# Seven late turnings by transposing transfers, EV on 128 rows, zero fills as steps, and a new order, in a recurrent attention + squared-ReLU kernel

## The chip, the cores and the metric

The kernel runs on one core of one Trainium2 chip. The metric is device microseconds of one execution, the median of three runs of the kernel before: 245.29 us (245.1 to 246.02). One further execution was profiled; its page and its trace are what is read below.

## The reference

For each of 4 batches and 8 heads, a 40x40 state is carried over 768 steps; its output feeds a two-layer network with squared ReLU.

```python
B, H, S, D = 4, 8, 768, 40
for t in range(S):
    y[:, :, t] = einsum('bhd,bhde->bhe', r_t, state)
    Sa = einsum('bhde,bhe->bhd', state, a_t)
    state = state * w_t[:, :, None, :] - einsum('bhd,bhe->bhde', Sa, b_t)
    state = state + einsum('bhd,bhe->bhde', v_t, k_t)
x = y.transpose(0, 2, 1, 3).reshape(B * S, H * D)      # 3072 x 320
h = maximum(x @ w_in, 0)                               # 320 x 2048
out = (h * h) @ w_out                                  # 2048 x 320
```

Inputs and output are float32; the kernel multiplies in bf16 and sums in float32.

## The kernel before, in words

The 768 steps are cut into 12 chunks of 64. A chunk is worked for all 32 (batch, head) pairs at once; 64 steps of two batches fill the 128 partitions. `load`, `prep`, `rec`, `read` and `ffn` add the steps of a chunk `c` to a plan, and `weights` adds the loads and casts of the network's weights. The names of the steps, with the chunk behind them:

- `ldw`, `ldk`, `ldb`, `ldv`, `lda`, `ldr`: the loads of a chunk, two transfers of 160 KB each, on SP's queue. `lwi` (8), `lwl` (1) and `lwo` (8): the weights; `cwi`, `cwl`, `cwo` cast them to bf16 (WIN, WLAST, WOUT). `st`: a chunk's store.
- `ln`, `hi`, `lo`, `ci`, `cf`, then `ei`, `ex`, `ef`, `eg`, `exw`: cumulative decay, by logarithm, a product with a triangle of ones on TensorE (PE) and an exponential. `castA`, `castR`, `castV`, `castB`, `castK`, `mulKB`: the inputs to bf16, keys and b scaled by the decay.
- Turnings: TK, TA, TR, TV, TS and XT transpose tiles on PE through an identity; `tK`, `tA`, `tR`, `tV`, `tS`, `xt` copy the result out of PSUM on ACT or DVE. TK turns KB (keys and b, [128, 32, 64]) into KBT; TV turns VU (v and u, same shape) into VUT; TS turns the state STb into Sb. In chunks 0 to 3 they work on 128x128 (line 397), later on 64-row halves, 32 matmuls each (line 394). BK turns back in chunks 0 to 2.
- EN, CX (lines 675 to 694): the two triangles, per half g, masked by `mEN`, `mCX` on DVE. AS: a times state. EV: first triangle times v, into the same PSUM slot; `u0` copies it; NU multiplies again by the triangle; `u1` writes the result u into the other 64 rows of VU.
- SC and S: the new state, scaled by `s` into STb. RS and Y: the output, from r times Sb (that is, the state of the chunk before) and from CX times keys; `y`, `yd` scale it, XT turns it.
- F (256 rows of w_in, line 390) and FL (its last 64 rows) per quarter u of the 2048 columns, `f` the ReLU, `q` the square, O the second product, `o` the copy out. In the last chunk O is three parts, OA, OB, OC.

A PE step has an array shape: 128*128 (F, O, whole turnings), 64*128 by row halves (FL, EN, CX, ci, cf, 64-row turnings), 128*64 by column halves (AS, SC, S, RS, Y), or 64*64 quadrants (EV, NU).

The order is written out: the string ORDER lists every step with its engine (`PE2` also names one of four PSUM slots), `Plan.issue` emits them in that order, and each engine works through its own entries in that order. A step's declared reads and writes become waits. PE's order is thus fixed: if the next step's input is late, PE stands. SP's queue is as strict: a transfer whose input is late holds those behind it. The buffers VU and KB are three deep (`NK`), most others two.

Ahead of the plan, constants are made and padding is zeroed on DVE and POOL (lines 312 to 323). One line each for a turning's matmul and its copy:

```python
pe(f"TV {c}", *tmode(c), ms, reads=VU0 + VU1, writes=[hb], alloc=[hb])
evac(f"tV {c}", lambda s, n, hb=hb: turned_pairs(VUT[q2], hb, c, s, n),
     1024, [hb], [("VUT", q2)], [hb])
```

Of the kernel before, what the change touches and what calls it, by code (L numbers as in the profile page):

```python
# [86 lines left out]
ORDER = """SP ldw 0; SP ldk 0; SP ldb 0; SP ldw 1; ACT ln 0; DVE hi 0; DVE lo 0; SP lda 0; PE0 cf 0; POOL  # L87
castB 0; SP ldk 1; POOL castK 0; ACT eg 0; PE1 TK 0; SP ldb 1; ACT ln 1; PE2 ci 0; DVE tK 0 g0;
ACT ef 0; SP ldv 0; DVE tK 0 g1; POOL hi 1; ACT exw 0; ACT castA 0; SP lda 1; DVE lo 1; PE1 TA 0;
ACT castB 1; PE2 ci 1; SP ldw 2; DVE tA 0 g1; DVE tA 0 g0; PE0 EN 0 g1; ACT exw 1; PE1 cf 1; POOL  # L90
castV 0 g1; DVE mEN 0 g1; ACT castK 1; SP ldr 0; POOL castV 0 g0; PE2 EN 0 g0; ACT ef 1; PE3 BK 0;
# [18 lines left out]
TV 2; PE2 TS 1; DVE s 2 q0; ACT tV 2; SP lwo 0 x2; DVE s 2 q1; PE0 F 0 u2; DVE tS 1; SP lwo 0 x3;  # L110
PE FL 0 u2; ACT castR 2; SP ldv 3; PE1 RS 1; PE Y 1; ACT castA 3; PE2 FL 0 u3; ACT f 0 u2; PE F 0
u3; DVE mulKB 3 h0; POOL mulKB 3 h1; PE3 TA 3; DVE y 1; ACT f 0 u3; PE0 TR 2; DVE yd 1; DVE tA 3
g0; PE1 XT 1; ACT tRw 2; SP ldr 3; PE2 TK 3; DVE xt 1; ACT cwo 0 x2; DVE tA 3 g1; POOL cwo 0 x3;
PE1 FL 1 u1; DVE tK 3; SP ldw 4; PE F 1 u1; POOL q 0 u1; PE3 CX 2 g1; ACT f 1 u1; PE0 CX 2 g0; DVE
mCX 2 g1; PE2 F 1 u2; ACT castV 3 g0; POOL castV 3 g1; SP lwo 0 x4; PE FL 1 u2; DVE mCX 2 g0; PE3
EN 3 g0; ACT f 1 u2; PE1 F 1 u0; POOL castR 3; SP lwo 0 x5; DVE mEN 3 g0; POOL q 0 u0; PE0 EN 3
g1; SP ldk 4; PE FL 1 u0; PE2 RS 2; DVE mEN 3 g1; PE Y 2; PE3 AS 3; ACT ln 4; ACT f 1 u0; PE0 FL 1
u3; DVE hi 4; PE EV 3; DVE yd 2; DVE lo 4; PE F 1 u3; ACT u0 3; POOL cwo 0 x4; DVE y 2; SP lda 4;
PE NU 3; ACT f 1 u3; PE2 ci 4 h0; POOL cwo 0 x5; DVE u1 3 g0; PE1 TS 2; ACT ex 4 h0 g1; SP ldb 4;
POOL q 0 u2; ACT ei 4 h0; DVE u1 3 g1; PE0 O 0 u0; ACT ex 4 h0 g0; ACT tS 2; PE2 ci 4 h1; POOL q 0  # L120
u3; PE3 TV 3; SP lwo 0 x6; ACT ex 4 h1 g0; ACT ei 4 h1; PE1 SC 3; DVE tV 3; ACT ex 4 h1 g1; SP lwo
0 x7; PE S 3 g0; PE S 3 g1; POOL castA 4; SP ldw 5; PE2 TR 3; DVE s 3 q1; PE O 0 u1; ACT tRw 3;
DVE s 3 q0; POOL mulKB 4 h0; PE3 XT 2; PE2 CX 3 g0; ACT xt 2; PE1 cf 4; DVE mCX 3 g0; PE O 0 u2;
ACT ef 4; SP ldv 4; DVE mulKB 4 h1; ACT cwo 0 x6; PE2 TA 4; PE1 CX 3 g1; POOL cwo 0 x7; DVE tA 4
g1; PE3 TK 4; DVE tA 4 g0; POOL q 1 u1; ACT tK 4; PE O 0 u3; DVE mCX 3 g1; PE2 F 2 u0; SP ldw 6;
DVE o 0; ACT q 1 u2; PE3 F 2 u2; DVE q 1 u0; ACT ln 5; PE0 EN 4 g0; PE FL 2 u2; DVE mEN 4 g0; PE1
FL 2 u3; POOL hi 5; ACT f 2 u2; PE FL 2 u0; SP ldr 4; PE F 2 u3; POOL lo 5; ACT f 2 u0; PE3 RS 3;
DVE f 2 u3; SP ldb 5; PE Y 3; POOL castV 4 g0; PE2 FL 2 u1; PE0 cf 5; DVE yd 3; POOL castV 4 g1;
DVE y 3; PE1 EN 4 g1; ACT ef 5; PE F 2 u1; POOL q 2 u0; DVE mEN 4 g1; PE3 XT 3; SP lda 5; ACT f 2
u1; PE0 TS 3; DVE xt 3; ACT ln 6; PE3 ci 5 h1; SP ldk 5; DVE tS 3; PE2 ci 5 h0; ACT ei 5 h1; PE1  # L130
AS 4; POOL hi 6; PE EV 4; ACT ex 5 h1 g1; POOL castR 4; ACT ei 5 h0; PE0 O 1 u0; DVE u0 4; ACT ex
5 h1 g0; POOL q 1 u3; SP lda 6; ACT ex 5 h0 g1; ACT ex 5 h0 g0; PE NU 4; PE O 1 u1; ACT u1 4 g0;
SP ldw 7; POOL lo 6; ACT u1 4 g1; PE2 SC 4; PE S 4 g0; PE S 4 g1; POOL castA 5; DVE mulKB 5 h1;
PE1 TR 4; PE3 ci 6 h1; ACT tR 4 g1; POOL mulKB 5 h0; SP ldr 5; PE O 1 u2; DVE s 4 q0; ACT ei 6 h1;
PE O 1 u3; ACT ex 6 h1 g0; DVE s 4 q1; SP ldv 5; ACT tR 4 g0; POOL q 2 u1; ACT ex 6 h1 g1; PE2 TS
4; ACT o 1; PE3 cf 6; DVE tS 4; PE1 TA 5; ACT ef 6; PE0 TV 4; SP ldr 6; DVE tA 5 g1; POOL castA 6;
PE2 TK 5; DVE tA 5 g0; ACT tV 4; PE3 FL 3 u1; POOL castR 5; PE F 3 u1; DVE tK 5; SP ldb 6; PE1 F 3
u0; DVE f 3 u1; ACT ln 7; PE FL 3 u0; PE0 TR 5; POOL castV 5 g0; ACT f 3 u0; PE2 EN 5 g0; SP lda
7; PE3 FL 3 u3; DVE mEN 5 g0; POOL q 2 u2; PE F 3 u3; ACT tR 5 g1; ACT tR 5 g0; PE1 CX 4 g0; PE2
# [77 lines left out]
def kernel(  # L217
# [99 lines left out]
    for v_ in [x[:, :, D:64] for x in KB + VU] + [x[:, :, :, D:64] for x in tR]:  # L317
        nc.vector.memset(v_, 0.0)
    for x in STb:
        nc.gpsimd.memset(x[:], 0.0)  # L320
# [766 lines left out]
```

## Time and profile before

| | us |
|---|---|
| median of three runs | 245.29 |
| profiled execution | 245.21 |
| its span, first to last instruction | 242.8 |
| PE busy | 223.2 |
| DVE busy | 182.8 |
| ACT busy | 178.8 |
| POOL busy | 119.9 |

The mean granted clock of PE is 0.993 of full speed. The difference between the profiled execution's time and its span, 2.4 us, lies around the program. A row of the timeline gives start, duration, engine, line, operation, `out<-in`, array shape, tile, count, and in brackets the idle time ahead and what ended it. A matmul's duration holds its way through the array, so that consecutive groups overlap: what a group costs PE is read from its start to the next group's start. A row of the page's groups gives the total busy time, the mean in ns, and the idle time ahead. A row of DMA issues gives count, KB of one, and the median us from issue to landing. `pb` is a PSUM slot, `SPq` is SP's queue at the issue of a transfer.

### The profile page before, as it was taken

How to read it: one execution, taken by the hardware profiler on the slowest of the kernel's cores; microseconds unless marked ns; L12 is line 12 of the kernel's file. 1: busy time of each engine (PE TensorE's matmuls, PEld its weight loads, DVE VectorE, ACT ScalarE, POOL GpSimd, SP SyncE). 2: the span in 40 equal slices, each digit the busy share in tenths (PEclk: the TensorE clock that was granted, in tenths of full speed). 3: DMA queues.
4: the chain of work that ended last, by engine and by line, in shares of the span. 5: the costliest groups of instructions: out<-in, count | busy, mean ns of one | idle time of the engine just before them, and what ended most of it. 6: DMA issues, size and time to landing. Idle time of an engine off the chain costs nothing.

```text
span 242.8 us, 12250 instructions
## 1 busy us (share of the span) xinstructions
PE 223.2 (92%) x5584; PEld 175.7 (72%) x5584; DVE 182.8 (75%) x227; ACT 178.8 (74%) x231; POOL 119.9 (49%) x110
## 2 busy tenths in 40 slices
PE   0587698899999999999999999999999999999994
...
DMA  6989899989978979997864957788457020000403
GB/s 144 232 165 211 191 248 188 227 186 209 196 182 135 196 160 185 184 178 143 173 113 95 223 117 121 186 143 153 106 109 136 6 57 5 3 5 0 100 11 107
DMA packets 102248, 33.54 MB, mean 138 GB/s; under 512 B 89014, under 2 KB 101814, under 8 KB 101942
## 3 DMA queue, kind: packets, MB, share of 16 engines
q1 hardware_dynamic: 101014, 32.45, 64.9%
...
q10 hardware_dynamic: 1184, 0.33, 0.6%
...
## 4 chain that ended last, share of the span: by engine, by line
PE 77%; SPq 9%; DMA 5%; ACT 2%; issue 2%; POOL 2%; DVE 1%; POOLq 0%; ACTq 0%
PE pb L390 66%; PE pb L394 7%; PE pb L397 4%; SPq L1003 2%; SPq L1011 2%; DMA raw_w<-in_w_dram 2%; DMA CX<-in_moe_w_in_dram 2%; SPq L453 2%; SPq L413 1%; SPq L421 1%; DMA raw_r<-in_r_dram 1%; DVE EN L689 1%; SPq L436 1%; POOL lo L384 1%; DVE CX L689 1%
## 5 line engine op out<-in xcount | busy, mean ns | idle before, releaser
L936 POOL TENSOR_TENSOR G<-G 128x1024 bf16<-128x1024 bf16 x24 | 45.7, 1909 | 32.2 <-ACT G L928 29.9
L390 PE MATMUL pb<-WOUT,G 128*128 128x320 bf16 (+1 forms) x400 | 57.0, 294 | 0.0
L928 ACT ACTIVATE G<-pb 128x1024 bf16<-128x1024 f32 x39 | 39.5, 1022 | 15.4 <-PE pb L390 15.3
L390 PE MATMUL pb<-XT,WIN 128*128 128x256 bf16 x384 | 48.4, 273 | 0.0
L390 PEld LDWEIGHTS <-G 128*128 128x128 bf16 x400 | 36.3, 98 | 13.7 <-issue 0.8
L390 PEld LDWEIGHTS <-WIN 128*128 128x128 bf16 x384 | 34.7, 98 | 8.1 <-issue 3.6
L689 DVE TENSOR_TENSOR CX<-pb,MSKI 128x1024 bf16<-128x1024 f32 x24 | 29.0, 1219 | 5.5 <-PE pb L390 5.4
L689 DVE TENSOR_TENSOR EN<-pb,MSK 128x1024 bf16<-128x1024 f32 x24 | 28.9, 1218 | 3.2 <-PE pb L390 3.0
L384 POOL TENSOR_TENSOR KB<-raw_kb,iG 128x640 bf16<-128x640 f32 x13 | 21.3, 1641 | 9.0 <-DMA raw_kb<-in_b_dram 8.3
L781 DVE TENSOR_TENSOR STb<-pb,GT 64x640 bf16<-64x640 f32 x22 | 18.0, 820 | 2.7 <-PE pb L390 2.4
L658 DVE TENSOR_TENSOR AR<-pb,GT 128x512 bf16<-128x512 bf16 x24 | 15.7, 686 | 5.2 <-PE pb L394 2.4
L384 POOL TENSOR_TENSOR lo<-lnW,hi 128x640 bf16<-128x640 f32 x9 | 13.2, 1466 | 11.4 <-ACT hi L376 11.0
L574 ACT ACTIVATE Gin<-pb 64x320 f32<-64x320 f32 x36 | 15.5, 429 | 4.3 <-PE pb L390 3.8
L390 PE MATMUL pb<-XT,WLAST 64*128 64x256 bf16 x192 | 17.1, 271 | 0.6 <-POOL WLAST L380 0.4
L390 PEld LDWEIGHTS <-EN 64*64 64x64 bf16 x768 | 14.8, 112 | 2.7 <-issue 1.6
L376 ACT ACTIVATE AR<-pb 128x512 bf16<-128x512 bf16 (+1 forms) x17 | 11.4, 694 | 6.7 <-PE pb L394 2.9
L859 DVE TENSOR_TENSOR Yb<-pb,Gin 128x640 bf16<-128x640 f32 (+1 forms) x24 | 12.4, 550 | 4.1 <-PE pb L390 4.1
L938 ACT ACTIVATE G<-G 128x1024 bf16<-128x1024 bf16 x15 | 15.5, 1052 | 0.0
L390 PE MATMUL pb<-UTI,hi 64*128 64x64 bf16 x192 | 8.2, 198 | 8.0 <-DVE hi L371 7.5
L930 DVE TENSOR_SCALAR G<-pb 128x1024 bf16<-128x1024 f32 x9 | 11.0, 1220 | 5.3 <-PE pb L390 5.3
L568 ACT ACTIVATE iG<-pb 128x640 f32<-128x640 f32 x18 | 12.5, 700 | 2.7 <-PE pb L390 2.5
L380 POOL CAST hi<-lnW 128x640 bf16<-128x640 f32 x7 | 5.0, 719 | 18.2 <-ACT lnW L532 9.5
...
## 6 DMA issues: line engine op xcount, KB each, us to landing
raw_kb<-in_k_dram SPq DMA_DIRECT2D x24, 160.0 KB, 4.4
raw_kb<-in_b_dram SPq DMA_DIRECT2D x24, 160.0 KB, 4.5
raw_a<-in_a_dram SPq DMA_DIRECT2D x24, 160.0 KB, 3.9
raw_v<-in_v_dram SPq DMA_DIRECT2D x24, 160.0 KB, 4.7
raw_w<-in_w_dram SPq DMA_DIRECT2D x23, 160.0 KB, 4.9
raw_r<-in_r_dram SPq DMA_DIRECT2D x22, 160.0 KB, 4.2
out_dram<-osb SPq DMA_DIRECT2D x22, 160.0 KB, 3.3
osb<-in_moe_w_out_dram SPq DMA_DIRECT2D x8, 320.0 KB, 6.1
```

What stands on the lines that cost most here:

```text
L384: return [("POOL", 40 + 2.35 * n, lambda: nc.gpsimd.tensor_tensor(out=o_(), in0=a_(), in1=b_(), op=op)), ("DVE", c_dve(n), lambda: nc.vect ...
L390: return lambda: nc.tensor.matmul(out=o_(), lhsT=l_(), rhs=r_(), start=start, stop=stop, skip_group_check=True)
L394: return lambda: nc.tensor.transpose(out=o_(), in_=i_(), identity=IDb[rows(g), :])
L568: ew(f"ei {c} h{jh}", [("ACT", c_act(2 * n), lambda hb=hb, jh=jh: nc.scalar.activation(out=iG[0][:].rearrange("p (g j) e -> p g (j e)", g= ...
L574: nc.scalar.activation(out=Gin[c % NGI][rows(g), NP * jh:NP * jh + NP, :].rearrange("p j e -> p (j e)"), in_=slot(hb, FP32)[rows(g), g, 0: ...
L658: ew(f"tA {c} g{g}", [("DVE", c_dve(512), lambda g=g: nc.vector.tensor_tensor(out=steps(AR[q2][:, 0, g]), in0=turned(ha, g), in1=steps(GT[ ...
L689: evac(f"m{nm} {c} g{g}", lambda s, n: [("DVE", c_dve(n), lambda: nc.vector.tensor_tensor(out=dst[q2][:, g, s].rearrange("p q i t -> p (q ...
L781: ew(f"s {c} q{q}", [("DVE", c_dve(2 * n), lambda q=q: nc.vector.tensor_tensor(out=STb[q2][rows(q), :, q, 0:D], in0=slot(hs, FP32)[rows(q) ...
L859: return [("DVE", c_dve(2 * (f1 - f0)), lambda: nc.vector.tensor_tensor(out=Yb[q2][:, :, to:to + f1 - f0], in0=slot(hy, FP32)[:, :, f0:f1] ...
L928: ("ACT", c_act(1024), lambda gb=gb, hf=hf: nc.scalar.activation(out=gb, in_=slot(hf, FP32)[:], func=ACTF.Relu)),
L936: ("POOL", 1900, lambda gv=gv: nc.gpsimd.tensor_tensor(out=gv, in0=gv, in1=gv, op=ALU.mult)),
L938: ("ACT", c_act(1024), lambda gv=gv: nc.scalar.activation(out=gv, in_=gv, func=ACTF.Square))],
```

## The change

1. Seven turnings go from PE to SP: TK and `tK` of chunk 11 become `dK 11`; TV and `tV` of 9, 10, 11 become `dV`; TS and `tS` of 8, 9, 10 become `dS`. Each is one transposing transfer from SBUF to SBUF of 128x2048 bf16. Sb is widened from 40 to 64 columns per head to take it.
2. EV of chunks 3 to 11 multiplies 128 rows instead of 64, in column halves. The added rows hold u's place in VU, which must be zero at that moment: two fills `zu c g` per chunk write those zeros ahead of it, on POOL or DVE, and EV reads them.
3. The zero fills of KB, VU, tR and STb at the start become steps of the plan (`zk`, `zv`, `zr`, `zs`) with an engine and a place in ORDER.
4. ORDER is new throughout: 1053 entries instead of 1032. The work of PE, ACT, DVE and POOL is dealt out anew.

The core of the diff, with ORDER up to the first FL and from the first transposing transfer on:

```diff
-2; PE2 EN 1 g0; PE0 TV 0; ACT castB 2; DVE mEN 1 g0; POOL castA 2; SP ldw 3; PE3 S 0 g0; ACT tV 0;
...
-DVE tK 2 g0; ACT ln 3; PE NU 1; SP ldv 2; ACT tS 0; PE2 CX 0 g0; POOL hi 3; DVE mCX 0 g0; PE1 TA
-2; POOL lo 3; SP lwl 0; ACT u1 1 g0; PE0 SC 1; DVE tA 2 g1; ACT u1 1 g1; PE S 1 g0; PE2 Y 0; DVE
...
-PE0 ci 3 h0; PE3 ci 3 h1; DVE bK 2; PE2 AS 2; ACT ei 3 h1; PE EV 2; DVE cwi 0 k1h1; POOL cwl 0;
-ACT ei 3 h0; PE1 F 0 u0; SP lwo 0 x1; ACT u0 2; ACT ex 3 h0 g0; PE FL 0 u0; SP ldr 2; ACT ex 3 h0
...
+ORDER = """SP ldw 0; SP ldb 0; SP ldk 0; POOL zv 1; POOL zr 0; SP ldk 1; ACT ln 0; SP ldb 1; POOL hi 0; ACT
+castB 0; POOL zr 1; DVE lo 0; SP ldw 1; DVE castK 0; PE0 cf 0; DVE zs 0; PE1 TK 0; DVE zk 0; ACT
+eg 0; SP lda 0; PE2 ci 0; POOL castB 1; DVE tK 0 g0; SP ldr 0; DVE zv 0; DVE castK 1; SP ldv 0;
...
+DVE tV 0; POOL zu 3 g0; ACT ef 2; SP lwo 0 x0; PE2 TA 2; POOL castV 1 g0; ACT exw 2; SP lwi 0
+k0 x2; DVE tA 2 g1; PE0 CX 0 g0; POOL zu 3 g1; PE1 AS 1; ACT castR 1; SP lwi 0 k0 x1; DVE mCX 0
+g0; PE EV 1; SP lwi 0 k0 x0; SP ldv 2; DVE tA 2 g0; PE0 CX 0 g1; ACT u0 1; PE3 TK 2; DVE mCX 0 g1;
+ACT ln 3; PE NU 1; PE2 TR 1; ACT hi 3; POOL cwi 0 k1h0; DVE tK 2 g1; PE0 TS 0; ACT u1 1 g0; SP lwi
+0 k0 x3; POOL cwi 0 k1h1; DVE tK 2 g0; ACT u1 1 g1; SP lwl 0; ACT tRw 1; POOL lo 3; PE1 Y 0; SP
...
+2; POOL cwi 0 k0h1; ACT ei 3 h0; DVE bK 2; PE EV 2; ACT ex 3 h0 g1; PE0 ci 3 h1; ACT ex 3 h0 g0;
+DVE u0 2; PE2 CX 1 g0; ACT ex 3 h1 g1; PE3 F 0 u0; SP lda 3; ACT ei 3 h1; DVE cwl 0; ACT ex 3 h1
+g0; DVE mCX 1 g0; PE NU 2; PE0 F 0 u2; ACT u1 2 g0; SP lwo 0 x1; SP ldk 3; ACT u1 2 g1; PE2 CX 1
+g1; PE FL 0 u2; DVE mCX 1 g1; PE FL 0 u0; PE1 FL 0 u1; ACT f 0 u0; PE F 0 u1; DVE f 0 u2; PE2 RS
...
+h1; ACT ex 10 h1 g0; SP dS 8; PE3 XT 7; DVE o 6; PE0 TK 9; ACT xt 7; POOL castV 10 g0; PE1 ci 10
...
+yd 8; ACT ei 10 h0; DVE y 8; ACT ex 10 h0 g1; PE2 cf 10; POOL mulKB 10 h0; SP st 6; PE3 EN 9
+g1; ACT ef 10; PE FL 7 u0; DVE mEN 9 g1; PE1 F 7 u2; SP ldk 11; POOL zu 11 g0; ACT f 7 u0; PE2 TA
...
+u2; ACT f 8 u3; PE FL 8 u2; SP ldr 10; PE2 AS 9; DVE f 8 u2; PE EV 9; PE1 ci 11 h1; ACT u0 9; PE0
+FL 7 u1; PE3 EN 10 g1; ACT ex 11 h1 g1; PE NU 9; DVE mEN 10 g1; SP ldr 11; ACT ei 11 h1; PE F 7
...
+FL 8 u1; PE1 ci 11 h0; DVE f 8 u0; SP dV 9; PE0 SC 9; ACT ex 11 h0 g0; PE S 9 g0; ACT ex 11 h0 g1;
...
+O 7 u0; DVE s 9 q1; ACT f 8 u1; PE O 7 u1; POOL castR 10; ACT q 8 u1; POOL q 7 u3; SP dK 11; PE2
...
+SP dS 9; PE O 7 u3; POOL q 8 u2; ACT q 8 u0; DVE tA 11 g0; DVE zu 11 g1; PE0 AS 10; ACT o 7; DVE
+tA 11 g1; PE EV 10; POOL castV 11 g0; PE3 CX 9 g1; ACT u0 10; PE2 TR 10; DVE mCX 9 g1; PE1 CX 9
+g0; POOL castR 11; PE NU 10; ACT u1 10 g0; DVE mCX 9 g0; PE3 O 8 u0; ACT u1 10 g1; PE O 8 u1; ACT
+tR 10 g1; ACT tR 10 g0; SP dV 10; PE0 RS 9; PE Y 9; PE2 SC 10; DVE y 9; PE S 10 g0; PE S 10 g1;
+PE1 TR 11; DVE yd 9; SP st0 0; DVE s 10 q1; PE O 8 u2; ACT tR 11 g0; ACT tR 11 g1; DVE s 10 q0;
+PE0 EN 11 g1; PE1 EN 11 g0; DVE mEN 11 g1; PE2 XT 9; PE O 8 u3; ACT xt 9; DVE mEN 11 g0; PE2 F 9
+u0; ACT o 8; PE FL 9 u0; PE1 CX 10 g0; ACT f 9 u0; PE3 CX 10 g1; DVE mCX 10 g0; PE0 AS 11; PE EV
+11; PE2 F 9 u2; ACT u0 11; DVE mCX 10 g1; PE NU 11; DVE q 9 u0; PE3 RS 10; ACT u1 11 g0; PE Y 10;
+ACT u1 11 g1; PE1 FL 9 u1; DVE yd 10; DVE y 10; PE F 9 u1; PE FL 9 u2; SP dV 11; PE3 XT 10; PE0 FL
+9 u3; ACT f 9 u2; DVE xt 10; PE F 9 u3; PE2 F 10 u2; ACT f 9 u3; SP dS 10; PE3 FL 10 u3; ACT f 9
+u1; PE FL 10 u2; PE F 10 u3; ACT f 10 u2; DVE q 9 u1; PE1 F 10 u0; DVE q 9 u2; ACT q 9 u3; POOL q
+10 u2; PE2 O 9 u0; DVE f 10 u3; SP st 7; PE FL 10 u0; PE0 CX 11 g1; ACT f 10 u0; PE3 CX 11 g0; DVE
+mCX 11 g1; PE O 9 u1; POOL q 10 u0; DVE mCX 11 g0; PE O 9 u2; PE0 RS 11; PE Y 11; PE O 9 u3; DVE
...
+    DTK, DTV, DTS = range(11, 12), range(9, 12), range(8, 11)
+    EVC = range(3, 12)
...
-    Sb = buf("Sb", [128, NJ, 2, D], BF16, 2)
+    Sb = buf("Sb", [128, NJ, 2, 64], BF16, 2)
...
-    for v_ in [x[:, :, D:64] for x in KB + VU] + [x[:, :, :, D:64] for x in tR]:
-        nc.vector.memset(v_, 0.0)
-    for x in STb:
-        nc.gpsimd.memset(x[:], 0.0)
...
+    for i in range(NK):
+        zeros(f"zk {i}", KB[i][:, :, D:64], 380, 500, [("KB", i, 0), ("KB", i, 1)])
+        zeros(f"zv {i}", VU[i][:, :, D:64], 380, 500,
+              [(x, i, g) for x in ("VU0", "VU1") for g in range(2)])
+    for i in range(2):
+        zeros(f"zr {i}", tR[i][:, :, :, D:64], 220, 300, [("tR", i)])
+        zeros(f"zs {i}", STb[i][:], 912, 1800, [("STb", i, 0), ("STb", i, 1)])
...
+    def turn(name, out_, in_, reads, writes):
+        plan.add(name, [("SP", 750)], ("ew", {"SP": lambda: nc.sync.dma_start_transpose(
+            out=out_(), in_=in_())}), reads=reads, writes=writes)
...
+            if c in EVC:
+                ew(f"zu {c} g{g}", [(e, d, lambda q=q, g=g: q.memset(
+                    VU[c % NK][rows(g), NJ * g:NJ * g + NJ, :], 0.0))
+                    for e, d, q in (("POOL", 700, nc.gpsimd), ("DVE", 500, nc.vector))],
+                   writes=[("VU1", c % NK, g)])
...
+        if c in DTK:
+            turn(f"dK {c}", lambda: KBT[q2][:].rearrange("p j x t -> p j (x t)"),
+                 lambda: KB[c % NK][:].rearrange("p h e -> p (h e)"), KBK, [("KBT", q2)])
...
-                                 lambda p=p, q=q, g=g: EN[q2][rows(1 - g), g, q, p, :],
-                                 lambda p=p, q=q, g=g: vu[rows(1 - g), NJ * g + 2 * p + q, 0:D],
+                                 lambda p=p, q=q, g=g: (EN[q2][:, g, q, p, :] if c in EVC else
+                                                        EN[q2][rows(1 - g), g, q, p, :]),
+                                 lambda p=p, q=q, g=g: vu[:, NJ * g + 2 * p + q, 0:D]
+                                 if c in EVC else vu[rows(1 - g), NJ * g + 2 * p + q, 0:D],
...
+            if c in DTS:
+                turn(f"dS {c}", lambda: Sb[q2][:].rearrange("p i q e -> p i (q e)"),
+                     lambda: STb[q2][:].rearrange("p i q e -> p (i q e)"),
+                     [("STb", q2, 0), ("STb", q2, 1)], [("Sb", q2)])
+                return
...
+        if c in DTV:
+            turn(f"dV {c}", lambda: VUT[q2][:].rearrange("p j x t -> p j (x t)"),
+                 lambda: vu[:].rearrange("p h e -> p (h e)"), VU0 + VU1, [("VUT", q2)])
```

270 lines of the change are left out of this document (127 added, 143 removed).

## The prediction

> **What bounds the kernel now.** I read the page first, for the engine that is busy and the chain that ends last, then the windows, for where that engine is not busy, then PE's timeline for the price of the pieces.
>
> ```profile
> span 242.8 us, 12250 instructions
> PE 223.2 (92%) x5584; PEld 175.7 (72%) x5584; DVE 182.8 (75%) x227; ACT 178.8 (74%) x231; POOL 119.9 (49%) x110
> PE   0587698899999999999999999999999999999994
> DMA  6989899989978979997864957788457020000403
> q1 hardware_dynamic: 101014, 32.45, 64.9%
> PE 77%; SPq 9%; DMA 5%; ACT 2%; issue 2%; POOL 2%; DVE 1%; POOLq 0%; ACTq 0%
> ```
> ```profile
> 0.00:46.40 46.40, 30.84 (x794) 24.95 (x794) 35.71 (x54) 30.02 (x37) 21.61 (x35) 0.96 0.93 196
> 60.00:220.00 160.00, 159.45 (x4289) 124.76 (x4281) 127.58 (x148) 126.34 (x169) 92.15 (x71) 1.00 0.64 126
> 220.00:242.80 22.80, 19.36 (x188) 14.80 (x186) 7.68 (x11) 10.66 (x12) 0.00 (x0) 1.00 0.23 58
> ```
> The windows (length, then PE, weight loads, DVE, ACT, POOL busy, granted clock, DMA share, GB/s) split the run in two. Up to 46.4 us PE is busy 30.84 of 46.4 us while the DMA engines are 0.93 busy: transfers set that part. From 60 us on PE is busy 159.45 of 160 us, with DVE, ACT and POOL at 80%, 79% and 58%, and from 220 us it works until the last store. So after the first part a microsecond of PE work is a microsecond of time, and work of the other engines is worth nothing unless PE waits for it.
>
> **The change, part by part.** The prices are PE's starts, one group to the next.
>
> ```profile
> 182.47 0.63 PE L394 MATMUL pb<-IDb,STb 64*128 64x64 bf16 x32
> 183.03 0.68 PE L390 MATMUL pb<-NZ,EN 64*64 64x40 bf16 x32
> 194.41 0.41 PE L394 MATMUL pb<-IDb,tA 64*128 64x64 bf16 x16
> 194.65 0.40 PE L390 MATMUL pb<-AR,VUT 64*128 64x64 bf16 x16
> 194.98 0.48 PE L390 MATMUL pb<-STb,AR 128*64 128x80 bf16 x16
> 195.39 0.68 PE L390 MATMUL pb<-VU,EN 64*64 64x40 bf16 x32
> 196.00 0.64 PE L394 MATMUL pb<-IDb,KB 64*128 64x64 bf16 x32
> 200.09 0.48 PE L390 MATMUL pb<-Sb,AR 128*64 128x80 bf16 x16
> 200.40 0.66 PE L390 MATMUL pb<-KB,CX 128*64 128x40 bf16 x32
> 200.91 0.44 PE L390 MATMUL pb<-STb,IDQ 128*64 128x320 bf16 x4
> 201.18 0.66 PE L390 MATMUL pb<-VU,KB 128*64 128x40 bf16 x32
> 201.78 0.64 PE L394 MATMUL pb<-IDb,VU 64*128 64x64 bf16 x32
> 202.25 0.34 PE L394 MATMUL pb<-IDb,Yb 64*128 64x64 bf16 x12
> 202.53 2.35 PE L390 MATMUL pb<-WOUT,G 128*128 128x320 bf16 x16
> ```
> *Seven turnings leave PE* (TK 11, TV 9 to 11, TS 8 to 10). Each is 32 matmuls of 64x64. TV 10 takes 201.78 to 202.25 = 0.47 us before a group of the same array shape, TS 8 0.56 us before another shape. I take 7 x 0.47 = 3.3 us, the change of shape counted next; bounds 3.2 and 3.9.
>
> *Changes of array shape.* The same 16 matmuls of 64 columns take 0.24 us (194.41 to 194.65) before their own shape and 0.33 us (194.65 to 194.98) before another; the 32 of the state's product with keys, 128x40, take 0.60 us (201.18 to 201.78) before another shape, against 0.51 us for the equal group at 200.40 before its own. A change of shape costs 0.09 us. Reading PE's entries in both orders, with EV of chunks 3 to 11 now in AS's shape (128*64), I count 198 changes before and 185 after: 13 x 0.09 = 1.2 us.
>
> *EV on 128 rows* keeps its 32 matmuls of 40 columns. EV in quadrants took 195.39 to 196.00 = 0.61 us up to another shape; the 128-row form takes the 0.60 and 0.51 us just read. Cost nothing; bounds -0.1 and +0.1 us each. One rule of the Trainium skill speaks against it: "TensorE: Matmul & The Clock Gate", section Part 3: Packing small matmuls, says that a weight load overlaps running matmuls only where the row groups differ, and 128-row loads share all of them. By it the nine EV would get longer than in quadrants; the rows of the two forms, equal within 0.1 us, go against it, and the sum stands.
>
> *Zero fills.* EV now also waits for the zeros `zu`, 18 fills (64x1024) in chunks 3 to 11, and the start's fills become steps.
>
> ```profile
> L320 POOL MEMSET STb<- 128x2048 bf16 x2 | 3.6, 1805 | 0.4 <-POOLq L1071 0.3
> L318 DVE MEMSET KB<- 128x384 uint32 x3 | 1.1, 378 | 0.1
> L376 ACT ACTIVATE VUT<-pb 128x2048 bf16<-128x2048 bf16 x6 | 11.3, 1876 | 3.4 <-PE pb L397 1.7 <-PE pb L394 1.6
> L371 DVE COPY VUT<-pb 128x2048 bf16<-128x2048 bf16 x6 | 7.3, 1221 | 3.0 <-PE pb L397 2.1 <-PE pb L394 0.9
> L371 DVE COPY Sb<-pb 128x1280 bf16<-128x1280 bf16 x5 | 4.1, 823 | 3.2 <-PE pb L394 2.9 <-PE pb L397 0.3
> ```
> By the STb fill 1024 columns are 0.9 us on POOL, by the KB fill 0.5 us on DVE: 13 x 0.9 and 5 x 0.5 = 14 us of engine time. It is paid for by the seven copies out of PSUM that go with the turnings (0.8 to 1.9 us each, some 8 us off DVE and ACT) and by POOL's idle 42%. The fills stand one to several steps ahead of their EV, so I cost them at nothing; if that cover fails, PE waits up to 0.9 us each.
>
> *The transposing transfers.* Each moves 128x2048 bf16, 512 KB, on SP's queue, and no such transfer is in the trace. The nearest rows:
>
> ```profile
> raw_kb<-in_k_dram SPq DMA_DIRECT2D x24, 160.0 KB, 4.4
> osb<-in_moe_w_out_dram SPq DMA_DIRECT2D x8, 320.0 KB, 6.1
> 183.65 1.92 PE L390 MATMUL pb<-XT,WIN 128*128 128x256 bf16 x16
> 218.93 0.48 PE L390 MATMUL pb<-Sb,AR 128*64 128x80 bf16 x16
> ```
> From issue to landing 160 KB takes 4.4 us and 320 KB 6.1 us, so 512 KB about 8.1 us, in a busy queue; a lone store's order of 4 us is the other end. What must cover it is the PE work between release and use. The shortest is dV 11: after NU 11 the new order has RS 10, Y 10, FL and F groups, O 9 u0 and FL 10 u0 ahead of CX 11, by the rows 0.3 + 0.6 + 6 x 0.3 (FL, the WLAST row further down) + 5 x 0.95 (F, half of the 16 below) + 0.3 + 2.3 = 10.1 us, less some 1.5 us in which the two u1 copies follow NU 11: 8.6 us. dV 10 has some 12, dV 9 and dK 11 over 15 us, counted alike. So at 4 to 8.1 us all seven are hidden, narrowly at the upper end, and I take no wait. In SP's queue dS 8 stands ahead of ldk 11, ldb 11, ldr 10 and ldr 11, whose readers come more than 10 us later; the DMA digits fall to 0 at slice 32 (188 us). The skill's pages differ on the path's speed: the Trainium skill's "VectorE: DVE Perf Modes", section The three transpose paths, gives 1309 ns for one 128x128 on this path, 16 of which would by estimate be 21 us; "Advanced Engine Details and Errata", section X-Bar Transpose (TRN2), calls them as fast as ordinary transfers. No run here shows either; the slow one is a rival below.
>
> *The first part, reordered.*
>
> ```profile
> 35.45 5.76 SPq L1003 DMA_DIRECT2D CX<-in_moe_w_in_dram  x2
> 43.21 2.00 SPq L1025 DMA_DIRECT2D osb<-in_moe_w_out_dram  x2
> 45.36 1.04 POOL L380 CAST WLAST<-CX 128x1024 bf16<-128x1024 f32 x1 [1.57 <-DMA CX<-in_moe_w_in_dram]
> 46.45 0.39 PE L390 MATMUL pb<-XT,WLAST 64*128 64x256 bf16 x4 [0.41 <-POOL WLAST L380]
> 43.99 0.69 DVE L371 CAST WIN<-G 128x1024 bf16<-128x1024 f32 x1
> 48.83 1.21 DVE L689 TENSOR_TENSOR CX<-pb,MSKI 128x1024 bf16<-128x1024 f32 x1
> ```
> The first FL waits at 46.45 for WLAST, whose bytes land at 45.3. Counting SP's entries, both orders have 18 chunk loads and 8 `lwi` ahead of `lwl`, the new one also `lwo 0 x0`, 328 KB: at the window's 196 GB/s +1.7 us. The cast goes to DVE (0.69 instead of 1.04 us), and CX 1 g1 must wait for the cast and for mCX 1 g0 (1.2 us), because both use one PSUM slot and mCX 1 stands behind the cast on DVE. So CX 1 g1 starts near 45.3 + 1.7 + 0.7 + 1.2 = 48.9 and the first FL at 49.2, 2.8 us later, but with NU 2 (0.6), one more F (1.0) and two CX (0.7) done ahead, 2.3 us. Net +0.5 us; bounds -1.3 (if `lwo`'s bytes fit into gaps) and +2. The earlier `hi 0` and the earlier k 1, b 1, r 0 and k 2 let PE reach this place sooner, which is worth nothing while the weights set it.
>
> *Other moves.* 160 us with 0.55 us of PE idle leave the new order nothing to win by better filling, so its own waits can only add: 0 to 3 us, I take 0. The strided copy into the wider `Sb` I cost at the same 0.82 us.
>
> **The sum.** 245.2 (profiled execution; 242.8 span and 2.4 around it; the median of the runs is 245.3) - 3.3 - 1.2 + 0.5 = 241.2 us. Own range: 245.2 - 3.9 - 1.3 - 1.3 = 238.7 to 241.2 + 3 = 244.
>
> **Rivals.**
> 1. *The start wins too.* The 15.6 us of PE idle ahead of 46.4 shrink because k 2, r 0 and b 1 come ahead of the weights, and more of PE's work than 2.3 us gets done there. For it: PE waits all over this stretch; against it: the DMA share of 0.93. The price is the bound -1.3 instead of +0.5: 239.4 us.
> 2. *The saved time comes back as waits.* Every chunk's EV now needs two more steps from POOL or DVE, and PE's order was rebuilt. Against: the idle above. A wait of 0.3 us in each of 12 chunks eats 3.6 us: 244.8 us, no measurable change.
> 3. *The turnings are slow (slower than before).* Six of them (dV 9, dK 11, dS 9, dV 10, dV 11, dS 10) go through one queue between NU 9 (up to 183.65) and RS 11 (218.93): 35.3 us. If each holds the queue for T, PE waits 6T - 35 us; at T = 8.1, the landing time above taken as serial, 13 us: 254 us. It decides from T = 35.3/6 + 4.0/6 = 6.6 us. For it: 512 KB is more than any transfer in the trace. Against: q1 moved 101014 packets in 64.9% of 16 engines' span, 25 ns of one engine each, so 2048 rows of 256 bytes would take 3.2 us on 16 engines; only much smaller pieces pass 6.6 us. By the skill's 21 us it would be near 330 us.
> 4. *The 128-row EV is slow*, its loads not overlapped: nine EV of 32 loads would add at most the 112 ns of a load row each, 32 us: 273 us. The rows of the equal form leave it almost no chance.
>
> ```profile
> L390 PEld LDWEIGHTS <-KB 128*64 128x64 bf16 x352 | 7.6, 112 | 0.9 <-issue 0.3
> ```
>
> **How the numbers follow.** Forecast 0.56, rival 1 0.12, rival 2 0.16, rival 3 0.14, rival 4 0.02. About 0.5%, 1.2 us, is what a measurement of this kernel can tell from no change. Faster: the forecast and rival 1, and a little of rival 2, 0.71; same: most of rival 2, 0.12; slower: rivals 3 and 4 and the rest of 2, 0.17. The range runs from 237.8, 1 us below the own range's end for a start that wins more than its bound, past rival 2 to 246.5, short of rival 3.
>
> **What would show it.** Right: no turnings by PE after the ones named, PE busy within 1 us of 160 from 60 to 220 us, the last PE group some 4 us earlier, transfers landing under 8 us with no PE wait for KBT, VUT or Sb, the first FL near 49 us. Wrong: PE idle ahead of CX 9 to 11, EN 11 or RS 9 to 11 with a DMA as releaser (rival 3); EV groups over 0.7 us (rival 4); many short PE waits for POOL or DVE (rival 2); a first FL before 46 us (rival 1).

## The result, and the profile after

The changed kernel takes 242.95 us (median of 4 runs, 241.4 to 243.8) against 245.66 us for the kernel before on the same chip: a ratio of 0.9867, 95% interval 0.9823 to 0.9911. In a second set of runs it was 0.9869 (0.9791 to 0.9947). The forecast was 241.2 us, its range 237.8 to 246.5; the gain is 2.7 us instead of 4.0. The profiled execution took 243.15 us, 241.4 of them span. The part around the span, 2.4 us in the kernel before, is 1.7 to 1.8 us in all four runs of the kernel after; no row shows why, and the forecast had kept it at 2.4. So 0.7 us of the gain comes from a place that nobody priced.

The page after, and its windows (columns as before):

```profile
span 241.4 us, 11825 instructions
PE 219.8 (91%) x5360; PEld 173.8 (72%) x5360; DVE 185.1 (77%) x237; ACT 171.9 (71%) x225; POOL 119.3 (49%) x117
DMA  6989999997979987888783878978994857093413
q1 hardware_dynamic: 115574, 36.13, 75.7%
```
```profile
0.00:46.40 46.40, 30.67 (x802) 25.53 (x802) 34.73 (x52) 27.64 (x35) 24.86 (x42) 0.89 0.90 195
60.00:220.00 160.00, 159.04 (x4065) 123.77 (x4062) 131.94 (x161) 127.52 (x171) 87.78 (x71) 1.00 0.80 152
220.00:241.40 21.40, 17.03 (x210) 13.42 (x208) 7.00 (x11) 5.24 (x7) 4.40 (x3) 0.96 0.26 63
```

PE has 224 instructions fewer, the seven times 32 of the turnings, and is 3.4 us less busy. In the middle it is as full as before (159.04 of 160 us; 157.86 in the repetition below). The last 80 O matmuls start at 228.13 us, 2.3 us earlier than before (230.47), where the prediction said some 4 us. q1 moved 14560 packets more, some 2080 for each transfer, about the 2048 pieces of 256 bytes that the prediction assumed; their time is (75.7% x 241.4 - 64.9% x 242.8) / 7 = 3.6 us of all 16 engines each, where 3.2 was estimated; with the repetition's 73.7% of 241.7 us it is 2.9. From slice 32 on the DMA digits fall to 0 in one slice only, before in six.

The timeline rows of the places that were priced (start, duration, engine, line):

```profile
47.28 0.69 DVE L383 CAST WLAST<-CX 128x1024 bf16<-128x1024 f32 x1 [0.46 <-DMA CX<-in_moe_w_in_dram]
49.36 0.41 PE L402 MATMUL pb<-AR,VUT 64*128 64x64 bf16 x16 [0.30 <-DVE CX L713]
49.59 0.62 PE L402 MATMUL pb<-XT,WLAST 64*128 64x256 bf16 x8
181.51 0.48 PE L402 MATMUL pb<-STb,AR 128*64 128x80 bf16 x16
181.81 0.66 PE L402 MATMUL pb<-VU,EN 128*64 128x40 bf16 x32
182.41 0.31 PE L402 MATMUL pb<-hi,UTI 64*128 64x320 bf16 x2
185.73 1.90 SPq L483 DMA_TRANSPOSE VUT<-VU  x1
210.34 1.87 SPq L483 DMA_TRANSPOSE VUT<-VU  x1
212.31 3.74 SPq L483 DMA_TRANSPOSE Sb<-STb  x1
217.23 0.63 PE L402 MATMUL pb<-AR,VUT 64*128 64x64 bf16 x32
```
```profile
L633 POOL MEMSET VU<- 64x1024 bf16 x13 | 12.3, 946 | 0.7 <-ACT XT L388 0.6
L633 DVE MEMSET VU<- 64x512 uint32 x5 | 2.4, 485 | 0.7 <-issue 0.5
```

The first FL starts at 49.59 us (forecast 49.2). EV takes 181.81 to 182.41 = 0.60 us, and AS ahead of it, now of EV's shape, 0.30 instead of 0.41 us. The fills take 12.3 + 2.4 = 14.7 us of POOL and DVE (forecast 14). A transposing transfer alone in the queue holds SP for 1.8 to 2.0 us, one right behind another for 2.8 and 3.7, and dS 8 in the busy queue at 168 us for 4.5. The last row is CX 11: it starts 6.9 us after the issue of dV 11 (210.34), and CX 10 starts 7.7 us after the issue of dV 10 (197.97 to 205.69). PE waits for neither.

The prediction's two halves are easily told apart by one number, the time from the first FL to the end of the span: 242.8 - 46.45 = 196.35 us before. The forecast put it at 241.2 - 2.4 - 49.2 = 189.6 us; the profiled execution shows 241.4 - 49.59 = 191.8 us, 2.2 us more. With the first FL 0.4 us later than forecast, the span is 2.6 us over the forecast; the 0.7 us saved around the span hide a part of that in the total. The same number is used for the experiments.

### The profile page after: what moved, and what is told of

Its sections match the earlier page's. It is cut to its first block, busy times and chain, and to the rows that moved or that the text cites. A ratio compares the mean times of both kernels' runs of the same rounds, so it can differ in the third digit from the quotient of the medians.

```text
span 241.4 us, 11825 instructions
## 1 busy us (share of the span) xinstructions
PE 219.8 (91%) x5360; PEld 173.8 (72%) x5360; DVE 185.1 (77%) x237; ACT 171.9 (71%) x225; POOL 119.3 (49%) x117
## 3 DMA queue, kind: packets, MB, share of 16 engines
q1 hardware_dynamic: 115574, 36.13, 75.7%
## 4 chain that ended last, share of the span: by engine, by line
PE 74%; DMA 8%; SPq 7%; DVE 4%; ACT 3%; issue 2%; POOL 1%; POOLq 0%; ACTq 0%
PE pb L402 65%; PE pb L406 6%; DMA G<-in_moe_w_in_dram 4%; PE pb L409 3%; DMA osb<-in_moe_w_out_dram 2%; SPq L433 2%; SPq L1048 2%; DMA raw_w<-in_w_dram 2%; SPq L425 1%; DVE AR L682 1%; POOL WIN L392 1%; SPq L465 1%; DVE VU L385 1%; ACT lnW L548 1%; ACT VU L388 1%
## 5 line engine op out<-in xcount | busy, mean ns | idle before, releaser
L973 POOL TENSOR_TENSOR G<-G 128x1024 bf16<-128x1024 bf16 x22 | 41.8, 1910 | 28.4 <-ACT G L965 23.4
L965 ACT ACTIVATE G<-pb 128x1024 bf16<-128x1024 f32 x36 | 36.0, 1021 | 11.1 <-PE pb L402 9.6
L396 POOL TENSOR_TENSOR KB<-raw_kb,iG 128x640 bf16<-128x640 f32 x10 | 15.8, 1580 | 16.7 <-ACT iG L584 14.9
L392 POOL CAST VU<-raw_v 64x640 bf16<-64x640 f32 x17 | 13.3, 785 | 13.3 <-DMA raw_v<-in_v_dram 12.8
L896 DVE TENSOR_TENSOR Yb<-pb,Gin 128x128 bf16<-128x128 f32 (+1 forms) x24 | 12.3, 553 | 9.5 <-PE pb L402 9.4
L396 POOL TENSOR_TENSOR lo<-lnW,hi 128x640 bf16<-128x640 f32 x7 | 9.8, 1402 | 16.4 <-DVE hi L383 16.2
L402 PEld LDWEIGHTS <-EN 64*64 64x64 bf16 (+1 forms) x768 | 14.5, 111 | 3.4 <-issue 2.2
L388 ACT ACTIVATE VU<-pb 64x640 bf16<-64x640 f32 x17 | 11.8, 697 | 7.1 <-PE pb L402 4.0
L967 DVE TENSOR_SCALAR G<-pb 128x1024 bf16<-128x1024 f32 x12 | 14.4, 1212 | 1.8 <-PE pb L402 1.8
L388 ACT ACTIVATE VUT<-pb 128x2048 bf16<-128x2048 bf16 x6 | 11.3, 1876 | 5.4 <-PE pb L406 3.1
```

The source lines that it names most:

```text
L388: alts.append(("ACT", c_act(n), lambda: nc.scalar.activation(out=o_(), in_=i_(), func=ACTF.Copy, scale=1.0 if scale is None else scale)))
L392: lambda: nc.gpsimd.tensor_copy(out=o_(), in_=i_())))
L396: return [("POOL", 40 + 2.35 * n, lambda: nc.gpsimd.tensor_tensor(out=o_(), in0=a_(), in1=b_(), op=op)), ("DVE", c_dve(n), lambda: nc.vect ...
L402: return lambda: nc.tensor.matmul(out=o_(), lhsT=l_(), rhs=r_(), start=start, stop=stop, skip_group_check=True)
L965: ("ACT", c_act(1024), lambda gb=gb, hf=hf: nc.scalar.activation(out=gb, in_=slot(hf, FP32)[:], func=ACTF.Relu)),
L967: ("DVE", c_dve(1024), lambda gb=gb, hf=hf: nc.vector.tensor_scalar(out=gb, in0=slot(hf, FP32)[:], scalar1=0.0, scalar2=None, op0=ALU.max))],
```

## The experiments

Nine kernels ran. Each is compared with runs of the kernel before on the same chip; line numbers of the profiles differ by some lines between kernels, since the order is part of the program text.

### The kernel after, once more

> The kernel after, unchanged, so that the three kernels run with it have their base on the same chip: 242.95 us, 0.987 of the kernel before. Its first part is read again: a half-clock stretch of PE ahead of the first FL, as in its first profile, would put the first FL at 49.6 us, none at 48.3 us, as in the run with EV on 64 rows.

Measured: 0.9869 (0.9791 to 0.9947), median 243.1 us. The waits of PE, from 60 to 220 us, in the profiled executions of after and then of this repetition (engine, tile, line, releaser: us in total, times, longest):

```profile
PE pb L402 <- issue: 0.6, 2, 0.4
```
```profile
PE pb L402 <- issue: 1.2, 1, 1.2
PE pb L406 <- DVE AR L682: 0.4, 1, 0.4
PE pb L402 <- DVE G L971: 0.2, 1, 0.2
48.68 0.82 PE L402 MATMUL pb<-XT,WLAST 64*128 64x256 bf16 x12
53.92 0.19 PE L402 MATMUL pb<-UTI,hi 64*128 64x64 bf16 x1 [1.01 <-issue]
203.81 0.19 PE L402 MATMUL pb<-AR,KBT 64*128 64x64 bf16 x1 [1.25 <-issue]
```

Here the first FL is at 48.68 us, but the rest takes 241.7 - 48.68 = 193.0 us. The same program starts the first FL 0.9 us earlier and loses 1.2 us after it: its waits are not the same from one execution to the next. Two of them, 1.01 and 1.25 us, have no releaser that the profile shows ("issue"), and stand in the middle of a group. Up to the first FL four of the kernels below have the same steps as the kernel after, and with them six executions put it between 47.50 and 50.52 us. The granted clock ahead of it does not explain that, as the expectation had it: up to 46.4 us it was 0.89 in the execution with 49.59 us and also in the one with 47.50, and 1.00 here.

### The turnings back on PE

Two kernels put TK, TV and TS of the seven places back, with their copies; DTK, DTV and DTS are empty. In the first, a turning stands soon behind its input, without regard to whether its slot is still being read:

```diff
-DVE mCX 9 g0; PE3 O 8 u0;
...
+DVE mCX 9 g0; PE1 TK 11; DVE tK 11; PE1 TS 9; ACT tS 9; PE3 O 8 u0;
...
```

> The kernel after, with the seven turnings back on PE (each 32 matmuls of 64x64 and a copy out of PSUM on DVE or ACT, placed between its input and its reader in the new order); 190 changes of array shape instead of 187 in the kernel after. By the prediction's sum it takes 7 x 0.47 = 3.3 us more for the turnings and 3 x 0.09 = 0.3 us for the changes: 243.0 + 3.6 = 246.6 us, with PE about 159 of 160 us busy from 60 to 220 us. If instead the transfers' gain was spent again on waits for DVE and ACT, or the gain lies in the order, it is less than 1.5 us slower, under 244.5 us. If the seven copies that DVE and ACT get back also count, over 248 us.

Measured: 257.4 us, ratio 1.046 (1.040 to 1.052), 14.5 us over after: four times what the sum gives. Its PE timeline, and windows (last three columns: granted clock, DMA share, GB/s), from an execution of 260.0 us:

```profile
202.10 0.64 PE L405 MATMUL pb<-IDb,KB 64*128 64x64 bf16 x32 [1.31 <-DVE CX L712]
204.06 1.04 PE L405 MATMUL pb<-IDb,STb 64*128 64x64 bf16 x32 [1.32 <-DVE KBT L382]
214.68 0.64 PE L405 MATMUL pb<-IDb,VU 64*128 64x64 bf16 x32 [1.09 <-DVE EN L712]
217.99 1.03 PE L401 MATMUL pb<-XT,WIN 128*128 128x256 bf16 x8 [1.30 <-ACT XT L387]
229.34 0.64 PE L405 MATMUL pb<-IDb,STb 64*128 64x64 bf16 x32 [1.31 <-DVE VUT L382]
203.40:210.00 6.60, 5.94 (x66) 3.73 (x67) 0.61 (x1) 3.02 (x4) 0.00 (x0) 0.50 0.01 3
210.40:257.00 46.60, 39.12 (x748) 30.45 (x742) 22.48 (x28) 19.71 (x23) 7.96 (x4) 1.00 0.12 30
```

The turning of keys waits for mCX 9 to free its slot, the next for the first one's copy, and so on: 1.1 to 1.3 us each. From the second of them on PE ran 6.6 us at half clock. From its first FL (50.52 us) to the end this execution takes 15.8 us more than the first execution of after. The sum's 3.6, the waits (9.5 us instead of 0.8; these five are 6.3 of them) and half of the 5.94 us worked at half clock make 15.3 of that: this kernel measures bad places more than turnings. The execution is 2.6 us above the median, so the 14.5 us of the median have somewhat less of the same. The second puts each turning between two groups of F or O, with a slot free long before and after:

```diff
-PE1 O 7 u0; DVE s 9 q1; ACT f 8 u1;
...
-PE O 7 u1;
...
+PE3 TV 9; PE1 O 7 u0; DVE s 9 q1; DVE tV 9; ACT f 8 u1;
...
+PE0 TK 11; DVE tK 11; PE O 7 u1;
...
```

> The kernel after with the seven turnings on PE again, now each between two groups of F or O, in a PSUM slot that has been free for over 1.6 us of PE work and isn't needed for 1.8 us more, their copies on DVE (tV 10 on ACT); 201 changes of array shape instead of 187. By the prediction's sum 7 x 0.47 + 14 x 0.09 = 4.6 us slower than the kernel after, 247.5 us, with no PE wait for KBT, VUT or Sb. If the copies out of PSUM (8 us of DVE and ACT) or the slots they hold matter as well, waits of PE come on top: over 249 us, as in the earlier run with the turnings back on PE (257.4 us). If the transfers' gain is spent elsewhere: under 245.5 us.

Measured: 248.4 us, ratio 1.014 (1.009 to 1.020), against 0.987 for after: 2.7% of 245 us or 6.7 us, with both intervals beside it 2.4 us either way. From the first FL to the end it takes 245.9 - 47.80 = 198.1 us, 6.3 us more than after and 5.1 more than its repetition. Rows of its PE timeline:

```profile
47.80 0.84 PE L401 MATMUL pb<-XT,WLAST 64*128 64x256 bf16 x12
169.00 0.64 PE L405 MATMUL pb<-IDb,STb 64*128 64x64 bf16 x32 [0.99 <-DVE CX L712]
188.07 0.64 PE L405 MATMUL pb<-IDb,VU 64*128 64x64 bf16 x32
188.65 1.26 PE L401 MATMUL pb<-WOUT,G 128*128 128x320 bf16 x8
221.90 0.41 PE L401 MATMUL pb<-AR,VUT 64*128 64x64 bf16 x16 [1.06 <-DVE G L966]
```

A turning takes 0.58 us with the change of shape behind it (188.07 to 188.65), as priced (0.47 + 0.09). The sum's 4.6 us and the two waits for DVE, 0.99 and 1.06 us, make 6.6 us. So the turnings' PE time is real. That the copies are not quite free, because DVE with more to do (191.9 us busy instead of 185.1) lets a slot and a ReLU come late, fits these two waits; it was not tested apart from the turnings.

### EV on 64 rows, no fills

All 18 fills leave the order; EV's line is that of the kernel before.

```diff
-    EVC = range(3, 12)
+    EVC = ()
-POOL zu 3 g0;
...
-POOL zu 3 g1;
...
```

> The kernel after, with EV of chunks 3 to 11 on 64 rows in quadrants again and without the 18 zero fills `zu`; 200 changes of array shape instead of 187. By the prediction's sum EV itself costs the same, the fills are hidden, and the changes cost 13 x 0.09 = 1.2 us: 244.2 us. If the fills or the 128-row loads cost PE something after all (rivals 2 and 4), this kernel is as fast as the kernel after or faster: 242.9 us or less.

Measured: 0.9876 (0.9811 to 0.9941), not to be told from 0.987. From the first FL (48.32 us) to the end it takes 241.2 - 48.32 = 192.9 us, 1.1 us more than after and 0.1 less than the repetition, and the interval of the ratio is 1.6 us either way: the total tells nothing. The 1.1 us alone would not show the price of the 13 changes (1.2 us) either, since PE's waits differ by as much (1.8 us here, 0.8 and 2.9 us there). With the waits taken off, PE's work is 0.9 to 1.3 us longer (table further down). The rows show where the changes lie:

```profile
48.32 0.83 PE L398 MATMUL pb<-XT,WLAST 64*128 64x256 bf16 x12
193.53 0.48 PE L398 MATMUL pb<-STb,AR 128*64 128x80 bf16 x16
193.94 0.68 PE L398 MATMUL pb<-VU,EN 64*64 64x40 bf16 x32
194.55 0.41 PE L398 MATMUL pb<-AR,VUT 64*128 64x64 bf16 x16
```

AS is back at 0.41 us, EV at 0.61. EV on 128 rows and its fills cost PE nothing that these traces show, and bring 0.1 us per chunk, which the time of the whole kernel can't show.

### EV on 128 rows alone, in the order before

```diff
-POOL castV 8 g0;
+POOL castV 8 g0; POOL zu 8 g0; POOL zu 8 g1;
```

(and alike in chunks 3 to 11; the fills of the start are ten steps at the head of the order, everything else is as in the kernel before)

> The kernel before, with its own order, EV of chunks 3 to 11 on 128 rows and the 18 fills `zu` on POOL, each pair behind its chunk's `castV`; 190 changes of shape instead of 199. By the prediction's sum 9 x 0.09 = 0.8 us faster than before: 244.9 us, POOL 16 us busier. If fills or loads cost PE: 245.7 us or more, with EV groups over 0.62 us or PE waits for `castV`, `mulKB` or `zu` on POOL.

Measured: 1.0077 (1.0036 to 1.0118), 1.9 us slower.

```profile
93.45 0.31 PE L402 MATMUL pb<-lo,UTI 64*128 64x320 bf16 x2 [1.32 <-POOL lo L396]
197.43 0.64 PE L406 MATMUL pb<-IDb,KB 64*128 64x64 bf16 x32 [1.02 <-POOL KB L396]
```

PE stands for `lo` and for `mulKB`, POOL steps that now come behind fills of 0.95 us each: `lo` starts at 92.01 us (90.05 before), behind a pair of fills at 84.35. From the first FL on the waits come to 3.4 us instead of 0.4; PE's work without them is 0.5 us shorter than before, where the sum said 0.8. The cover of the fills is a matter of their place: in the kernel after, whose order deals POOL's work out around them and gives 5 of the 18 to DVE, PE waits for neither.

### The transposing transfers alone, in the order before

```diff
-PE0 TV 11; POOL q 9 u1; DVE xt 10; PE1 TS 10; DVE tV 11; PE3 F 10 u2; ACT tS 10;
+SP dV 11; POOL q 9 u1; DVE xt 10; SP dS 10; PE3 F 10 u2;
```

(and alike at the other five; the fills of the start as in the kernel above)

> The kernel before, with its own order, in which the seven turnings and their copies are transposing transfers on SP's queue (each issued where the turning stood); 199 changes of shape, as before. The turnings' PE time is saved, 3.3 us, but dV 11 has only 1.9 us between u1 11 and CX 11 g0, dV 9 and dV 10 some 4.7 us, dS 10 stands behind dV 11 in the queue, ahead of RS 11. If a transfer lands about 4 us after its issue and holds the queue 2 us, PE waits 2 us at CX 11 and about 2 us at RS 11: 245.7 - 3.3 + 4 = 246.4 us, no gain. If it lands after 8 us, PE waits 6 us at CX 11, 3 us each at CX 9 and CX 10 and more at RS 11: about 255 us. If it lands in under 2.5 us: 243 us. The wait at CX 11 g0 gives the time from issue to landing directly.

Measured: 253.4 us, ratio 1.028 (1.021 to 1.035). SP's queue, PE's waits, and windows at and behind them, from an execution of 253.8 us:

```profile
187.47 4.23 SPq L479 DMA_TRANSPOSE VUT<-VU  x1
193.83 0.61 PE L398 MATMUL pb<-AR,VUT 64*128 64x64 bf16 x16 [3.43 <-DMA VUT<-VU]
218.70 2.00 SPq L479 DMA_TRANSPOSE VUT<-VU  x1
223.24 0.93 PE L398 MATMUL pb<-AR,VUT 64*128 64x64 bf16 x32 [2.00 <-DMA VUT<-VU]
192.60:199.40 6.80, 5.57 (x64) 3.56 (x64) 1.23 (x1) 1.97 (x2) 2.72 (x2) 0.51 0.53 105
223.40:226.80 3.40, 3.40 (x47) 2.37 (x42) 2.36 (x2) 0.35 (x1) 0.00 (x0) 0.50 0.52 97
```

The waits measure the landing. dV 11, alone in the queue, was issued at 218.70 and let PE go at 223.24: 4.5 us. dV 9, behind dS 8 and the two loads of ldb 11, took 187.47 to 193.83 = 6.4 us. Both lie inside the prediction's 4 to 8.1 us, and below the shortest cover in the kernel after (6.9 us). The 2 us of wait expected at CX 11 came, those at RS 11 did not; CX 9 waited 3.43 us. PE waited 5.4 us for the two, and worked 5.57 + 3.40 us at half clock from there on, which loses half of it, 4.5 us. With the turnings' 3.3 us saved that makes 6.6 us. The ratio gives 6.8 us (2.8% of 245), but this execution was 8.7 us over the median of before: its other waits, 2.9 us from the first FL on instead of 0.4, make up the rest. That a run of this kernel at a mean clock of 0.999 took 250.0 us and those at 0.97 to 0.98 took 250.9 to 254.1 us agrees in direction. In this order the transfers lose; 5 to 6.5 us between release and use are what these two landings would have needed.

### `lwo` behind `lwl`

```diff
-SP lwo 0 x0; PE2 TA 2;
...
-SP lwl 0; ACT tRw 1;
...
+PE2 TA 2;
...
+SP lwl 0; SP lwo 0 x0; ACT tRw 1;
```

(its cast `cwo 0 x0` behind `cwi 0 k0h1`)

> The kernel after with the first transfer of w_out (`lwo 0 x0`, 328 KB) behind `lwl` in SP's queue instead of ahead of four `lwi`, and its cast behind the casts of w_in. By the prediction's first-part term the 328 KB delay `lwl` by 1.7 us: the first FL comes 1.7 us earlier, and the kernel is up to 1.7 us faster, 241.3 us. If the bytes fitted into gaps, or the order of the recurrence sets the place where PE is, there is no difference, 242.9 us.

Measured: 0.9886 (0.9819 to 0.9952), no difference that can be told. The trace speaks against the 1.7 us:

```profile
38.63 1.14 SPq L1039 DMA_DIRECT2D CX<-in_moe_w_in_dram  x2
48.04 0.68 DVE L382 CAST WLAST<-CX 128x1024 bf16<-128x1024 f32 x1
50.54 0.82 PE L401 MATMUL pb<-XT,WLAST 64*128 64x256 bf16 x12
```

`lwl` is issued at 38.63 us (41.46 in after), and the cast of WLAST no longer waits for a transfer; still it starts at 48.04 us and the first FL at 50.54, as late as with `lwo` in its old place in another execution (50.52). Here PE and DVE themselves come late to this place. In the two executions of after the cast did wait for the transfer, 0.46 and 0.81 us, and that is the most that moving `lwo` could win there.

### Three more turnings on SP's queue

```diff
-    DTK, DTV, DTS = range(11, 12), range(9, 12), range(8, 11)
+    DTK, DTV, DTS = range(10, 12), range(8, 12), range(7, 11)
...
+SP ldk 9; SP dS 7; PE3 TA 8;
...
+DVE u1 8 g1; SP dV 8; ACT ex 9 h0 g0;
...
-PE0 TS 7; SP ldb 10; ACT o 5; PE1 TV 8; DVE tS 7;
+SP ldb 10; ACT o 5;
...
+POOL mulKB 10 h0; SP dK 10; SP st 6;
...
-DVE xt 8; PE2 TK 10;
+DVE xt 8;
```

> The kernel after with three more turnings on SP's queue (TS 7, TV 8, TK 10, the ones next in time), where the 16 DMA engines are 0.89 busy (140 to 180 us); 187 changes of shape, as after. By the price of a turning 3 x 0.47 = 1.4 us faster: 241.5 us, if 3.6 us more of the 16 engines' time each still fits between loads. If the busy queue delays the loads of chunks 10 and 11 or a transfer lands later than its cover (6.4 us were measured in a busy queue), PE waits for it and the kernel is slower than the kernel after, 243.5 us or more.

Measured: 0.9955 (0.9908 to 1.0003), 0.9% slower than after.

```profile
140.00:180.00 40.00, 36.88 (x906) 28.34 (x903) 31.40 (x41) 26.62 (x39) 25.12 (x21) 1.00 1.01 174
166.83 0.64 PE L400 MATMUL pb<-AR,VUT 64*128 64x64 bf16 x32 [1.03 <-DMA VUT<-VU]
196.09 0.41 PE L400 MATMUL pb<-AR,VUT 64*128 64x64 bf16 x16 [1.39 <-DMA VUT<-VU]
```

The 16 engines are full (share 1.01) from 140 to 180 us. The new dV 8 lands late, 6.35 us after its issue at 160.48, and so does dV 9 in a queue that has fallen behind (issued at 189.84 instead of 185.73): 2.4 us of waits eat the 1.4 us won. In this kernel the trick ends where the DMA engines have no room.

### One turning back: six transfers

```diff
-ACT u1 10 g1; PE O 8 u1; ACT tR 10 g1; ACT tR 10 g0; SP dV 10;
+ACT u1 10 g1; PE1 TV 10; PE O 8 u1; ACT tR 10 g1; ACT tR 10 g0; ACT tV 10;
```

> The kernel after with one of the seven turnings, TV 10, on PE again (between O 8 u0 and O 8 u1, its copy on ACT), so that no transposing transfer is under way from 196 to 209 us. Two executions of the kernel after show PE standing 0.41 and 1.25 us in EN 11 near 203 us with no releaser, 5 to 6 us after the issue of dV 10. If the stall comes of that transfer, it is gone, and the kernel takes 0.47 + 2 x 0.09 - (0.4 to 1.25) us, between 0.2 us slower and 0.6 us faster than the kernel after: 242.3 to 243.1 us. If it has nothing to do with it, the stall stays near EN 11 and the kernel is 0.65 us slower: 243.6 us.

Measured: 242.9 us, ratio 0.9925 (0.9889 to 0.9962): by the median as the first theory has it, by the ratio nearer to the second. EN 11 shows no stall in its trace (202.72 to 203.28 us), but neither does the kernel with `lwo` moved, which has all seven transfers. Whether the stall at EN 11 comes of dV 10 stays open.

## Why the prediction was right, and by how much it was off

One table checks the prices apart from the waits. It goes from the first FL to the start of the last 80 O matmuls; the waits in between, as the profile lists them, are taken off. The last column is the sum's: for the kernel after 183.6 - 3.3 - 1.2 - 2.3 (the work done ahead of the first FL), for the others 177.5, the middle of the two executions of after, with the change that was expected.

| kernel | first FL | last O group | waits | PE's work | by the sum |
|---|---|---|---|---|---|
| before | 46.45 | 230.47 | 0.4 | 183.6 | |
| after | 49.59 | 228.13 | 0.8 | 177.7 | 176.8 |
| after, once more | 48.68 | 228.84 | 2.9 | 177.3 | 176.8 |
| turnings between F and O groups | 47.80 | 233.26 | 2.7 | 182.8 | 182.1 |
| EV on 64 rows | 48.32 | 228.75 | 1.8 | 178.6 | 178.7 |
| three more turnings off PE | 47.50 | 228.88 | 5.2 | 176.2 | 176.1 |
| six transfers | 48.31 | 228.31 | 1.8 | 178.2 | 178.2 |
| `lwo` behind `lwl` | 50.54 | 229.99 | 1.6 | 177.9 | 177.5 |

The prices hold within 0.9 us in every row, and so the gain inside the span comes from the places that were priced. What the prices do not give is the waits, 0.8 to 5.2 us in the changed kernels.

*Seven turnings off PE, 3.3 us:* right. 0.58 us with one change of shape where they were put back; no wait of PE for KBT, VUT or Sb in the kernel after.

*Changes of shape, 1.2 us:* right in the rows (AS 0.41 to 0.30 us) and in the table (178.6 against 177.7 and 177.3). The prediction counted 198 and 185 changes in the orders, the experiments count 199 and 187, so that 12 or 13 are saved; the difference is 0.1 us.

*EV and the fills, nothing:* right for this order. In the order before, 18 fills on POOL cost waits of 1.32 and 1.02 us, so POOL's 42% of idle time was not the cover: the place in POOL's queue was. The prediction's other ground, that the fills stand one to several steps ahead of their EV, is the one that held.

*The transfers hidden:* right in the outcome, but with less room than was counted. They land after 4.5 us alone and 6.4 us in a busy queue. The covers were 6.9 us for dV 11 and 7.7 us for dV 10, where the prediction has 8.6 and some 12 us: for dV 11 it counts O 9 u0 at 2.3 us, which is the row of 16 matmuls, while one quarter is 8 of them and takes 1.2 us. At its own upper end, 8.1 us, these two and dS 10 (212.31 to RS 11 at 220.07, 7.8 us) would have landed too late. Rival 3 (6.6 us each, one behind the other) falls: two issued one behind the other held the queue for 1.87 and 3.74 us, and no transfer made PE wait in the kernel after. Its mechanism is real all the same, as the transfers in the order before (1.028) and three more of them (0.9955) show.

*The first part, +0.5 us:* the first FL came at 49.59 and 48.68 us, forecast 49.2; but the same steps gave 47.50 to 50.52 us in six executions, so that the agreement is partly luck. The cast of WLAST waited for its transfer as forecast, but for 0.46 and 0.81 us only; `lwo`'s 1.7 us is not the price, and moving it away gained nothing that can be told.

*The step that failed: "Other moves ... its own waits can only add: 0 to 3 us, I take 0".* This is the term that was mis-sized. From the first FL to the end the kernel after took 191.8 and 193.0 us, 2.2 and 3.4 us over the forecast's 189.6. In the kernel before, PE's waits after the first FL come to 0.4 us; in the first execution of after to 0.8 us, in the repetition to 2.9 us. The last store added 0.9 us in the first: it was issued at 237.40 and the span ended 4.0 us later; before, it was 239.73 and 3.1 us; in the repetition 0.5 us. That leaves 0.9 us of the one gap and 0.4 us of the other, which is PE's work in the table above the sum's 176.8 us and which no row explains. Rival 2 did not come: waits for another engine's result are 0.2 and 0.6 us, before 0.2. The rest of the waits, 0.6 and 2.3 us (before 0.2), are stalls with no releaser, whose cause stays open.

*Luck:* the profiled execution came out some 2 us over the forecast and not 2.6, because the time around the span fell from 2.4 to 1.7 us, which the prediction has no term for.
